# Seven-product feed-forward: two operand sums kept in PSUM, u's sums on GpSimd, token products by halves in one bank

## The chip, the cores and the metric

One Trainium2 chip, one of its cores. The metric is the device time of one launch in microseconds, as the median of the runs shown. A core has TensorE (PE in the profile; its weight loads are a row of their own, PEld), VectorE (DVE), ScalarE (ACT), GpSimd (POOL) and the queues that issue DMAs, SyncE's (SP) and ScalarE's among them. Each engine runs its own instructions in program order and waits on semaphores for the others.

## The reference

`x` is 8 sequences of 3008 tokens with 256 channels. A spectral filter (FFT over the tokens, a complex 256x256 product with bias, a soft threshold, inverse FFT) feeds a mixer:

```python
X = np.fft.rfft(x, axis=1)
Yr = Xr @ w_r - Xi @ w_i + b_r          # Yi likewise, then a soft threshold on both
x = np.fft.irfft(Y, n=x.shape[1], axis=1)
xt = x.transpose(0, 2, 1)
h = np.maximum(xt @ w_tok1, 0.0) @ w_tok2
u = x + h.transpose(0, 2, 1)
h2 = np.maximum(u @ w_ch1, 0.0) @ w_ch2
return (u + h2).astype(np.float32)
```

## The kernel before

Everything is kept transposed, channels on partitions and tokens in the free dimension. An fp32 product is made of three matmuls on halves of the words (`mm3`, lines 196 to 198: high by high, high by low, low by high), so every operand is first split into a high part (a cast, on ACT, line 146 or `high`, line 1112) and a low part (the value less its high part, line 149 or `lower` and `above`).

**Stages.** Until about 1125 us the spectral filter of all five units runs beside the feed-forward of the first two sequences. From then on `channel7` does the remaining six sequences, three units of two, in 18 chunks. A chunk is 1024 tokens wide (896 for the first of a unit) and is worked as two halves of h = 512 (448) columns. `u @ w_ch1` and the product with `w_ch2` are each seen as 2x2 blocks (two halves of the 256 channels by two halves of the tokens, and so on) and made with seven block products instead of eight. The operands of the first are seven sums of quarters of u (`b11`, `t1`, `t2`, `b21`, `b22`, `t3`, `t4`), split into high and low in tiles `ub`; those of the weights are made once, by `weigh` and `weigh2`.

**A step.** Each chunk has six steps, one for each pair of hidden blocks. `one(new, i)` makes first-layer product i, on the PSUM banks x, w and y (tiles `sx`, `sw`, `sy` in the profile); products 6, 7 and 4 add to bank x and product 3 to bank w. From the banks come the four blocks of the hidden layer and, after the ReLU, the seven operands of the second layer: `b11`, `b22`, `b21` and the sums `t1`, `t2`, `t4`, `t3` (tiles `ts`; the split operands are `op`). `two(old, i)` makes the second-layer products of the step before: 1, 5, 6, 7 and 2 gather in banks of their own (`po`), 3 and 4 go to bank y and are added to `uf` at once (`taken`). At a chunk's last step (`ends`) the gathered sums are added to `uf` and stored.

**Between the steps.** `make_u` (line 844) makes u for a group of up to 470 tokens: two halves of 128 channels, twelve large matmuls and some small ones, in bank x for the first half and bank y for the second, each copied by ACT to `uf` (line 867). The table `when` sets one group behind each of two or three steps of a chunk. `first_u` and `rest_u` (lines 1027 to 1042) make the operands of the next chunk behind the last two steps: four sums on DVE, and seven splits by `divide`, high on ACT and low on DVE.

**Order.** The program is written engine by engine in this order, and a scheduler then sets the order of the instructions on each engine, so products of the step before slip in between those of the new one. At run time each engine takes its list as it stands.

Two things in the code matter below. A PSUM bank is used by one engine at a time: the next writer or reader of bank x on another engine waits for the last. And `sn`, `ts`, `op`, `ub` are rings of 4, 4, 9 and 8 buffers.

Of the kernel before, what the change touches and what calls it, by code (L numbers as in the profile page):

```python
# [11 lines left out]
F32 = mybir.dt.float32  # L12
# [3 lines left out]
ALU = mybir.AluOpType  # L16
# [110 lines left out]
def tile_kernel(ctx: ExitStack, tc: tile.TileContext, io):  # L127
# [716 lines left out]
    def make_u(g):  # L844
        u, b, s0, k = groups[g]
        gh, gl = gts[u]
        w, b2 = wts.pop(g), b2s.pop(g)
        _, c0, c1 = span(g)
        n = c1 - c0
        homes = [m for m, (cu, at, cw) in enumerate(chunks) if cu == u and at < c1 and c0 < at + cw]  # L850
        for m in homes:
            if m not in ufs:
                ufs[m] = wc["uf"].tile([128, 2, CW7 if chunks[m][2] > CW else CW], F32, name="uf", bufs=3)
        for ct in range(2):
            cs = slice(ct * 128, (ct + 1) * 128)
            pt = wc["banks"]["xy"[ct]] if "banks" in wc else bank("pu")
            for jt in range(2):
                mm3(pt[:, :n], gh[:, jt, b, cs], gl[:, jt, b, cs], w[:, jt, :n], w[:, 2 + jt, :n], jt == 0, False)
            for s in range(k):
                PE.matmul(pt[:, s * TOKS:(s + 1) * TOKS], lhsT=b2[:, s, cs], rhs=g2[:, 0 if s0 + s == 0 else 1], start=False, stop=s == k - 1)  # L860
            if g == 0:
                us[0] = [wc["wk2"].tile([128, 2, CW], F32R, name=k) for k in ("uh", "ul")] if ct == 0 else us[0]
                S.copy(out=us[0][0][:, ct, :n], in_=pt[:, :n])
            for m in homes:
                _, at, cw = chunks[m]
                lo, hi = max(at, c0), min(at + cw, c1)
                S.copy(out=ufs[m][:, ct, lo - at:hi - at], in_=pt[:, lo - c0:hi - c0])
            if g == 0:
                V.tensor_tensor(out=us[0][1][:, ct, :n], in0=ufs[0][:, ct, :n], in1=us[0][0][:, ct, :n].bitcast(F32), op=ALU.subtract)
        return n  # L870
# [156 lines left out]
    def first_u(n):  # L1027
# [36 lines left out]
    def channel7(ns):  # L1064
# [46 lines left out]
        def high(new, k, src=None):  # L1111
            S.activation(out=new[3][k][:, 0], in_=new[4][k] if src is None else src, func=AF.Relu if k in ("b11", "b21") else AF.Copy)  # L1112
# [206 lines left out]
```

## Time and profile before

| | |
|---|---|
| median of 3 runs | 2544.31 us (2542.53 to 2550.55) |
| the profiled execution's own time | 2546.06 us |
| its span, first to last instruction | 2544.3 us |
| TensorE clock granted, mean | 0.989 |
| busy: PE, PEld | 2374.4 us (93%), 1988.2 us (78%) |
| busy: DVE, ACT, POOL | 1831.6 us (72%), 1398.1 us (55%), 1216.3 us (48%) |
| first product of `channel7` starts | 1125.4 us |
| DMA: HBM read, written | 177.57 MB, 97.39 MB |

A row of the groups of instructions gives the line, the engine, out<-in by the program's names, the shape, how often, busy time and mean duration in ns, and the idle time before with what ended it. A row of the timeline gives start and duration in us, and in brackets the idle time before and what ended it. Durations of matmuls overlap, so a matmul's price is read from start to start. A row of the waits gives who waited for whom, the total in us, how often, and the longest.

### The profile page before, as it was taken

What the parts mean: (1) busy time and instruction counts of PE and PEld (TensorE: products, weight loads), DVE (VectorE), ACT (ScalarE), POOL (GpSimd) and SP (SyncE); (2) the same over time, 40 slices, a digit from 0 to 9 for tenths busy, and PEclk for the clock granted to TensorE, in tenths of its full rate; (3) what the DMA queues carried; (4) which work ended last, traced back from release to release, by engine and by line L of the source; (5) the groups of instructions that cost most, each with busy time, mean ns of one, the idle gap of its engine ahead of it and who ended that gap; (6) DMA issues with size and microseconds to landing.
All of it is one profiled execution on the core that took longest, in us unless ns stands there. A gap on an engine that the chain in (4) does not pass through costs nothing.

```text
span 2544.3 us, 33504 instructions
## 1 busy us (share of the span) xinstructions
PE 2374.4 (93%) x12200; PEld 1988.2 (78%) x12200; DVE 1831.6 (72%) x2551; ACT 1398.1 (55%) x2492; POOL 1216.3 (48%) x905
## 2 busy tenths in 40 slices
PE   8999999999999999998998989989989899998887
PEld 7778989999888889887776767777767677776665
DVE  7876667655466645566788887788787878777886
ACT  6754445445344434345665665665665666665564
POOL 0001332323133323315767676676677766776766
PEclk9999999999999999998999999999999999999999
DMA  8864577656555554341121112212112121221100
GB/s 210 255 217 131 178 232 225 176 171 199 176 172 170 162 166 141 116 134 37 56 63 59 37 56 63 63 47 86 42 36 71 44 82 37 61 63 35 54 1 33
DMA packets 149762, 277.13 MB, mean 109 GB/s; under 512 B 10917, under 2 KB 94461, under 8 KB 149597
## 3 DMA queue, kind: packets, MB, share of 16 engines
q1 hardware_dynamic: 115209, 208.40, 27.8%
q10 hardware_dynamic: 34388, 66.60, 7.7%
q8 instruction: 96, 1.57, 0.3%
q14 instruction: 69, 0.57, 0.1%
HBM read 177.57 MB, written 97.39 MB: 108 GB/s over the span
## 4 chain that ended last, share of the span: by engine, by line
PE 44%; DVE 17%; POOL 15%; issue 14%; ACT 4%; DMA 3%; SPq 1%; DVEq 0%; ACTq 0%; POOLq 0%
POOL op L1101 11%; DVE sn L1101 3%; PE po L197 3%; PE po L196 3%; PE po L198 3%; POOL ts L1101 3%; PE px L482 2%; DVE ts L1101 2%; PE ph L196 2%; PE pm L198 2%; PE pm L196 2%; PE ph L198 2%; PE ph L197 2%; PE pm L197 2%; DVE ts L1104 2%
## 5 line engine op out<-in xcount | busy, mean ns | idle before, releaser
L1101 POOL TENSOR_TENSOR op<-ts,op 128x512 fp32r<-128x512 f32 (+1 forms) x432 | 618.1, 1451 | 0.0
L1112 ACT ACTIVATE op<-ts 128x512 fp32r<-128x512 f32 (+1 forms) x432 | 264.9, 619 | 257.8 <-DVE ts L1104 107.2
L1101 POOL TENSOR_TENSOR op<-sn,op 128x512 fp32r<-128x512 f32 (+1 forms) x108 | 166.4, 1541 | 493.7 <-ACT op L1112 439.2
L149 POOL TENSOR_TENSOR yl<-z,yh 128x512 fp32r<-128x512 f32 x72 | 95.9, 1332 | 272.6 <-ACT yh L146 266.5
L485 POOL TENSOR_TENSOR xf<-xf 128x256 f32<-128x256 f32 x84 | 68.6, 816 | 242.0 <-ACT xf L484 216.1
L1112 ACT ACTIVATE op<-sn 128x512 fp32r<-128x512 f32 (+1 forms) x216 | 134.6, 623 | 80.2 <-DVE sn L1101 77.2
L1101 DVE TENSOR_TENSOR sn<-sy,sn 128x512 f32<-128x512 f32 (+1 forms) x108 | 73.1, 676 | 139.0 <-ACT sn L1108 84.6
L149 DVE TENSOR_TENSOR xtl<-xf,xth 128x768 fp32r<-128x768 f32 x84 | 85.1, 1013 | 118.4 <-ACT xth L146 118.3
L1108 ACT COPY sn<-sx 128x512 f32<-128x512 f32 (+1 forms) x216 | 123.6, 572 | 60.2 <-PE sx L198 58.2
L899 DVE SCALAR_TENSOR_TENSOR hlo<-ph,hh 128x512 fp32r<-128x512 f32 (+3 forms) x156 | 98.6, 636 | 77.5 <-ACT hh L898 77.1
L196 PE MATMUL pm<-wmh,xth 128*128 128x256 f32 x504 | 146.1, 290 | 4.9 <-ACT xth L146 3.0
L1101 DVE TENSOR_TENSOR uf<-sy,uf 128x512 f32<-128x512 f32 (+1 forms) x216 | 144.8, 671 | 6.5 <-PE sy L198 6.4
L1101 POOL TENSOR_TENSOR ts<-sn 128x512 f32<-128x512 f32 (+1 forms) x108 | 148.9, 1379 | 0.0
L198 PE MATMUL pm<-wmh,xtl 128*128 128x256 f32 x504 | 142.4, 284 | 0.8 <-DVE xtl L149 0.8
L197 PE MATMUL pm<-wml,xth 128*128 128x256 f32 x504 | 142.3, 283 | 0.0
L898 ACT ACTIVATE hh<-ph 128x512 fp32r<-128x512 f32 (+3 forms) x156 | 86.3, 556 | 99.6 <-PE ph L198 91.5
L1101 DVE TENSOR_TENSOR ts<-sn,ts 128x512 f32<-128x512 f32 (+1 forms) x108 | 126.5, 1172 | 8.4 <-ACT op L1112 0.5
L196 PE MATMUL po<-op,ws 128*128 128x512 f32 (+1 forms) x324 | 128.9, 398 | 3.4 <-ACT op L1112 1.5
L197 PE MATMUL po<-op,ws 128*128 128x512 f32 (+1 forms) x324 | 128.3, 396 | 3.9 <-POOL op L1101 3.9
L1104 DVE SCALAR_TENSOR_TENSOR op<-sn,op 128x512 fp32r<-128x512 f32 (+1 forms) x108 | 107.5, 995 | 31.1 <-ACT op L1112 31.1
L198 PE MATMUL po<-op,ws 128*128 128x512 f32 (+1 forms) x324 | 127.4, 393 | 0.0
L196 PE MATMUL ph<-uh,w 128*128 128x512 f32 (+3 forms) x312 | 117.8, 379 | 3.8 <-DVE hlo L899 2.9
(243 smaller groups left out, 7592.4 us busy)
## 6 DMA issues: line engine op xcount, KB each, us to landing
wt<-wt_d SPq DMA_DIRECT2D x28, 940.0 KB, 5.7
x<-in_x SPq DMA_DIRECT2D x39, 480.0 KB, 4.6
wt<-ws_d SPq DMA_DIRECT2D x36, 512.0 KB, 4.4
a<-a_d SPq DMA_DIRECT2D x36, 512.0 KB, 5.6
b_d<-bt ACTq DMA_DIRECT2D x36, 512.0 KB, 5.7
a_d<-a ACTq DMA_DIRECT2D x36, 480.0 KB, 4.0
wt<-wt_d SPq DMA_DIRECT2D x21, 752.0 KB, 5.0
b<-b_d SPq DMA_DIRECT2D x32, 480.0 KB, 6.3
```

Source lines behind the costliest of these rows:

```text
L149: lo_eng.tensor_tensor(out=lo, in0=src, in1=hi.bitcast(F32), op=ALU.subtract)
L196: PE.matmul(out, lhsT=wh, rhs=xh, start=start, stop=False, skip_group_check=more)
L197: PE.matmul(out, lhsT=wh, rhs=xl, start=False, stop=False, skip_group_check=more)
L198: PE.matmul(out, lhsT=wl, rhs=xh, start=False, stop=stop, skip_group_check=more)
L482: PE.matmul(pt[:, o:o + 128], lhsT=x, rhs=f2cols(2 * kp + ab), start=True, stop=True)
L485: (V if plain else G).tensor_tensor(out=xf[:, 0], in0=xf[:, 1], in1=xf[:, 2], op=ALU.add)
L898: S.activation(out=hh, in_=pt, func=AF.Relu)
L899: V.scalar_tensor_tensor(out=hlo, in0=pt, scalar=0.0, in1=hh.bitcast(F32), op0=ALU.max, op1=ALU.subtract)
L1101: eng.tensor_tensor(out=out, in0=in0, in1=in1, op=op)
L1104: V.scalar_tensor_tensor(out=out, in0=in0, scalar=0.0, in1=in1, op0=MAX, op1=op)
L1108: S.copy(out=t, in_=banks[k][:, :new[2]])
L1112: S.activation(out=new[3][k][:, 0], in_=new[4][k] if src is None else src, func=AF.Relu if k in ("b11", "b21") else AF.Copy)
```

## The change

- **The sums in PSUM.** The first products' copies (`snap`) stay, but the sums for b11 and b22 are written back to banks y and w instead of to SBUF, and their ReLU copies on ACT go. `t1`, `t2` and the new `t3` are made by one DVE instruction each that takes the ReLU while it reads the bank; the low parts of b11 and b22 likewise. `t3` and b22's low part move from POOL to DVE. b21 is copied to SBUF by ACT with the ReLU, and its low part moves from DVE to POOL.
- **The order of products.** `two(old, 3)` comes ahead of `one(new, 6)`; 3 goes ahead of 2; `one(new, 4)` and what hangs on it come behind `two(old, 2)`.
- **Token products by halves.** `half_u` makes one half of a group, always in bank x, and the table sets one half (in a unit's first chunk two) behind a step; groups are fetched behind their second half.
- **u's sums on GpSimd.** Within `channel7` the low parts of `ub` and the sums `t1` to `t4` of u go to POOL. `weigh` and `weigh2` take their scratch from a pool of their own instead of from the `ub` ring.

```diff
-            pt = wc["banks"]["xy"[ct]] if "banks" in wc else bank("pu")
+        pt = wc["banks"]["x"] if "banks" in wc else bank("pu")
...
-        pool, w1 = wc["seven"], wc["w1"]
-        a = pool.tile([128, 2, 2, 2, 128], F32, tag="ub", name="a", bufs=8)
+        pool, w1 = wc["sums"], wc["w1"]
+        a = pool.tile([128, 2, 2, 2, 128], F32, tag="a", name="a")
...
-        split(ub[:, 0], ub[:, 1], src, S, V)
+        split(ub[:, 0], ub[:, 1], src, S, G if "tail" in wc else V)
...
-        V.tensor_tensor(out=t1, in0=b12, in1=b11, op=ALU.subtract)
+        (G if "tail" in wc else V).tensor_tensor(out=t1, in0=b12, in1=b11, op=ALU.subtract)
...
             if new:
+                sums(new, "t1", "t2", "t4", "t3")
+                X, W, Y = (b[k][:, :h] for k in "xwy")
                 one(new, 1)
-                v["b11"] = snap(new, "x")
-                one(new, 5)
-                v["b22"] = snap(new, "w")
+                x1 = snap(new, "x")
             if old:
                 two(old, 1)
...
             if new:
-                one(new, 6)
-                v["x2"] = snap(new, "x")
-                one(new, 2)
-                add(v["b11"], b["y"][:, :h], v["b11"])
-                high(new, "b11")
-                one(new, 3)
-                add(v["x2"], b["w"][:, :h], v["x2"])
-                S.activation(out=v["x2"], in_=v["x2"], func=AF.Relu)
-                one(new, 7)
-                add(v["b22"], b["x"][:, :h], v["b22"])
-                S.activation(out=v["b22"], in_=v["b22"], func=AF.Relu)
-                high(new, "b22")
+                one(new, 5)
+                w1 = snap(new, "w")
             if old:
                 two(old, 3)
                 taken(old, 3, 1)
             if new:
-                sums(new, "t1", "t2", "t4", "t3")
-                above(v["t1"], v["b11"], v["x2"], SUB)
-                add(v["t2"], v["b22"], v["t1"])
+                one(new, 6)
+                x2 = snap(new, "x")
+                one(new, 3)
+                add(x2, W, x2)
+                S.activation(out=x2, in_=x2, func=AF.Relu)
+                one(new, 2)
+                add(Y, Y, x1)
+                high(new, "b11", Y)
+                one(new, 7)
+                add(W, X, w1)
+                above(v["t1"], Y, x2, SUB)
+                high(new, "b22", W)
+                lower(new, "b11", Y)
+                above(v["t2"], W, v["t1"], ADD)
                 high(new, "t1")
             if old:
                 two(old, 5)
-            if new:
-                one(new, 4)
-                high(new, "b21", b["x"][:, :h])
-                above(v["t4"], b["x"][:, :h], v["t2"], SUB)
-                above(new[3]["b21"][:, 1], b["x"][:, :h], new[3]["b21"][:, 0].bitcast(F32), SUB)
-                high(new, "t2")
-                high(new, "t4")
-                lower(new, "t1")
-                add(v["t3"], v["b22"], v["x2"], G, SUB)
-                above(new[3]["b11"][:, 1], v["b11"], new[3]["b11"][:, 0].bitcast(F32), SUB)
-                high(new, "t3")
-                for k in ("b22", "t2", "t4", "t3"):
-                    lower(new, k)
...
+            if new:
+                one(new, 4)
+                v["b21"] = single()[:, :h]
+                S.activation(out=v["b21"], in_=X, func=AF.Relu)
+                above(v["t4"], X, v["t2"], SUB)
+                high(new, "b21")
+                lower(new, "b22", W)
+                above(v["t3"], W, x2, SUB)
+                high(new, "t2")
+                high(new, "t4")
+                high(new, "t3")
+                for k in ("t1", "b21", "t2", "t4", "t3"):
+                    lower(new, k)
...
-                spots = [(m - 2, half - len(mine) + 1 + i) for i in range(len(mine) - 1)] + [(m - 1, 3)]
+                spots = [(m - 2, half - 2), (m - 2, half - 1), (m - 1, 0), (m - 1, 1)][4 - 2 * len(mine[1:]):] + [(m - 1, 2), (m - 1, 3)]
```

What the scheduler makes of it, at three places. First DVE in one step without token products, from the addition that takes bank w's sum to the two `taken` (in the names, `sn<-sw,sn` is that addition, `op` a low part, `ts` a sum). Before:

```order
L1101 TENSOR_TENSOR sn<-sy,sn 128x512
L1104 SCALAR_TENSOR_TENSOR op<-sn,op 128x512
L1101 TENSOR_TENSOR sn<-sw,sn 128x512
L1101 TENSOR_TENSOR sn<-sx,sn 128x512
L1101 TENSOR_TENSOR uf<-sy,uf 128x512
L1104 SCALAR_TENSOR_TENSOR ts<-sn 128x512
L1101 TENSOR_TENSOR ts<-sn,ts 128x512
L1101 TENSOR_TENSOR uf<-sy,uf 128x512
L1104 SCALAR_TENSOR_TENSOR ts<-sx,ts 128x512
L1104 SCALAR_TENSOR_TENSOR op<-sx,op 128x512
```

And after:

```order
L1111 TENSOR_TENSOR sn<-sw,sn 128x512
L1111 TENSOR_TENSOR sy<-sy,sn 128x512
L1111 TENSOR_TENSOR sw<-sx,sn 128x512
L1114 SCALAR_TENSOR_TENSOR ts<-sy,sn 128x512
L1114 SCALAR_TENSOR_TENSOR op<-sy,op 128x512
L1114 SCALAR_TENSOR_TENSOR ts<-sw,ts 128x512
L1114 SCALAR_TENSOR_TENSOR op<-sw,op 128x512
L1114 SCALAR_TENSOR_TENSOR ts<-sx,ts 128x512
L1114 SCALAR_TENSOR_TENSOR ts<-sw,sn 128x512
L1111 TENSOR_TENSOR uf<-sy,uf 128x512 x2
```

Ten instructions become eleven, and the three that read SBUF alone (`op<-sn,op`, `ts<-sn`, `ts<-sn,ts`) are gone: each of the eleven reads a bank. The second place is PE around the token products of a chunk's later step (`sx<-wt`, `sy<-wt` and the small `g`, `b` products are a group's two halves). Before:

```order
L196 MATMUL po<-op,w2h 128x512
L197 MATMUL po<-op,w2h 128x512
L196 MATMUL sx<-wt_14397,gh 128x470
...
L860 MATMUL sx<-g_79,b_14399 128x94 x5
L196 MATMUL sy<-wt_14397,gh 128x470
...
L860 MATMUL sy<-g_79,b_14399 128x94 x5
L196 MATMUL sx<-ub,w_963 128x448
```

And after:

```order
L198 MATMUL po<-op,ws_10466 128x512
L196 MATMUL sx<-wt_12485,gh 128x470
...
L864 MATMUL sx<-g_79,b_12487 128x94 x5
L196 MATMUL sw<-ub,ws 128x512
L197 MATMUL sw<-ub,ws 128x512
L196 MATMUL po<-op,ws_10466 128x512
L197 MATMUL po<-op,ws_10466 128x512
L198 MATMUL po<-op,ws_10466 128x512
L196 MATMUL sx<-ub,w_963 128x512
```

One half stands there now, and between it and the next step's first product in bank x stand five matmuls on other banks. The third place is POOL from one chunk's `uf<-t` to the next's. Before, each step has six instructions and nothing lies between the steps; after it reads:

```order
L1042 TENSOR_TENSOR t<-uf 128x512
L1111 TENSOR_TENSOR op<-ts,op 128x512
...
L1048 TENSOR_TENSOR t<-uf 128x512
L1049 TENSOR_TENSOR t<-t,uf 128x512
L1050 TENSOR_TENSOR t<-uf,t 128x512
...
L149 TENSOR_TENSOR ub<-t,ub 128x512 x2
L149 TENSOR_TENSOR ub<-uf,ub 128x512 x2
L149 TENSOR_TENSOR ub<-t,ub 128x512 x2
L1111 TENSOR_TENSOR op<-ts,op 128x512
L1111 TENSOR_TENSOR op<-sn,op 128x512
```

A step has five instructions there now (`op<-ts,op`, `op<-sn,op` and three more `op<-ts,op`), and ten of u's low parts and sums stand between the steps, six of them in a row ahead of the low parts of the chunk's last step.

More of the change, by code (lines that the diff above doesn't have):

```diff
@@ L842, in load_b2, with home, half_u @@
         b2s[g] = b2
-    def make_u(g):
+    def home(g):
+        u = groups[g][0]
+        _, c0, c1 = span(g)
+        found = [(m, at, cw) for m, (cu, at, cw) in enumerate(chunks) if cu == u and at < c1 and c0 < at + cw]
+        for m, _, cw in found:
+            if m not in ufs:
+                ufs[m] = wc["uf"].tile([128, 2, CW7 if cw > CW else CW], F32, name="uf", bufs=3)
+        return c0, c1, found
+    def half_u(g, ct):
         u, b, s0, k = groups[g]
         gh, gl = gts[u]
-        w, b2 = wts.pop(g), b2s.pop(g)
-        _, c0, c1 = span(g)
+        w, b2 = wts[g], b2s[g]
+        c0, c1, found = home(g)
@@ L870, in make_u @@
-        return n
+        cs = slice(ct * 128, (ct + 1) * 128)
+        pt = wc["banks"]["x"] if "banks" in wc else bank("pu")
+        for jt in range(2):
+            mm3(pt[:, :n], gh[:, jt, b, cs], gl[:, jt, b, cs], w[:, jt, :n], w[:, 2 + jt, :n], jt == 0, False)
+        for s in range(k):
+            PE.matmul(pt[:, s * TOKS:(s + 1) * TOKS], lhsT=b2[:, s, cs], rhs=g2[:, 0 if s0 + s == 0 else 1], start=False, stop=s == k - 1)
+        if g == 0:
+            us[0] = [wc["wk2"].tile([128, 2, CW], F32R, name=k) for k in ("uh", "ul")] if ct == 0 else us[0]
+            S.copy(out=us[0][0][:, ct, :n], in_=pt[:, :n])
@@ L872, in split_u, with make_u @@
+        for m, at, cw in found:
+            lo, hi = max(at, c0), min(at + cw, c1)
+            S.copy(out=ufs[m][:, ct, lo - at:hi - at], in_=pt[:, lo - c0:hi - c0])
+        if g == 0:
+            V.tensor_tensor(out=us[0][1][:, ct, :n], in0=ufs[0][:, ct, :n], in1=us[0][0][:, ct, :n].bitcast(F32), op=ALU.subtract)
+        if ct:
+            del wts[g], b2s[g]
+    def make_u(g):
+        for ct in range(2):
+            half_u(g, ct)
+        return groups[g][3] * TOKS
     def split_u(n):
@@ L1111, in high, with lower @@
         def high(new, k, src=None):
-            S.activation(out=new[3][k][:, 0], in_=new[4][k] if src is None else src, func=AF.Relu if k in ("b11", "b21") else AF.Copy)
-        def lower(new, k, eng=G):
-            add(new[3][k][:, 1], new[4][k], new[3][k][:, 0].bitcast(F32), eng, SUB)
+            S.activation(out=new[3][k][:, 0], in_=new[4][k] if src is None else src, func=AF.Copy if k[0] == "t" else AF.Relu)
+        def lower(new, k, src=None):
+            lo, hi = new[3][k][:, 1], new[3][k][:, 0].bitcast(F32)
+            if src is None:
+                add(lo, new[4][k], hi, G, SUB)
+            else:
+                above(lo, src, hi, SUB)
         def taken(old, i, q):
```

50 lines of the change are left out of this document (17 added, 33 removed).

## The prediction, on record before the changed kernel ran

> **What bounds the kernel now.** I read the page's head, then the stages, the waits of the later stage, and one step's timeline. The stages first (us, busy time of PE, PEld, DVE, ACT and POOL, granted clock, DMA):
>
> ```profile
> 150.00:1125.00 975.00, 960.34 (x5704) 867.75 (x5703) 596.13 (x889) 450.07 (x770) 252.33 (x218) 1.00 0.56 172
> 1125.00:2544.30 1419.30, 1278.84 (x5747) 1007.87 (x5745) 1114.20 (x1409) 848.97 (x1545) 962.48 (x682) 0.98 0.17 52
> 1175.00:1200.00 25.00, 16.94 (x50) 11.64 (x49) 17.29 (x27) 10.34 (x21) 8.64 (x7) 0.71 0.00 0
> ```
>
> Until 1125 us PE is full, and the change touches nothing there but `weigh`'s scratch. In the 1419 us of `channel7` every engine has idle time: PE 140 us by busy time, and more in truth, since a matmul's shown end overlaps the next. So I count PE by starts. A 512-wide matmul starts every 0.23 us, a 448-wide one every 0.205, and one half of a 470-token group takes 2.42 us (1602.95 to 1605.37):
>
> ```profile
> 1611.89 0.40 PE L196 MATMUL po<-op,ws 128*128 128x512 f32 x1
> 1612.12 0.39 PE L197 MATMUL po<-op,ws 128*128 128x512 f32 x1
> 1612.35 0.39 PE L198 MATMUL po<-op,ws 128*128 128x512 f32 x1
> ...
> 1612.90 0.36 PE L197 MATMUL sx<-ub,w 128*128 128x448 f32 x1
> 1613.11 0.36 PE L198 MATMUL sx<-ub,w 128*128 128x448 f32 x1
> ```
>
> ```profile
> 1602.95 0.48 PE L196 MATMUL sx<-wt,gh 128*128 128x470 f32 x1 [0.69 <-DVE op L1104]
> ...
> 1605.37 0.46 PE L196 MATMUL sy<-wt,gh 128*128 128x470 f32 x1
> ...
> 1605.62 0.55 ACT L867 COPY uf<-sx 128x470 f32<-128x470 f32 x1 [0.87 <-PE sx L860]
> ```
>
> A step has 14 products of three matmuls: 42 x 0.23 = 9.66 us, or 8.61 at 448. There are 90 and 18 steps, and by these rows (each half has two such matmuls, and bank y as many as x) 44 halves of 470 tokens and 36 of 376:
>
> ```profile
> L1101 DVE TENSOR_TENSOR sn<-sy,sn 128x512 f32<-128x512 f32 x90 | 61.9, 687 | 106.4 <-ACT sn L1108 61.8 <-PE sy L198 44.5
> L196 PE MATMUL sx<-wt,gh 128*128 128x470 f32 x44 | 18.5, 420 | 17.0 <-DVE op L1104 17.0
> L196 PE MATMUL sx<-wt,gh 128*128 128x376 f32 x36 | 13.6, 379 | 6.9 <-DVE op L1104 6.9
> ```
>
> PE's floor: 90 x 9.66 + 18 x 8.61 + 44 x 2.42 + 36 x 1.95 (scaled by width) = 869 + 155 + 106 + 70 = **1200 us** of 1419. The other 219 us are what the change can win. Who keeps PE waiting, from 1300 to 2480 us (total, times, longest):
>
> ```profile
> PEld sx L196 <- DVE op L1104: 54.9, 48, 2.7
> PEld sx L196 <- ACT sn L1108: 47.4, 108, 1.3
> PEld sy L196 <- DVE uf L1101: 30.7, 27, 2.0
> PEld sy L196 <- DVE sn L1101: 24.6, 20, 1.9
> ```
>
> Nearly all waits are for a bank (x, y) that DVE or ACT still reads. Why DVE is late shows in one step:
>
> ```profile
> 1684.75 1.79 DVE L1101 TENSOR_TENSOR ts<-sn,ts 128x512 f32<-128x512 f32 x1
> ...
> 1685.96 1.72 POOL L1101 TENSOR_TENSOR op<-ts,op 128x512 fp32r<-128x512 f32 x1
> ...
> 1687.00 0.68 DVE L1104 SCALAR_TENSOR_TENSOR ts<-sx,ts 128x512 f32<-128x512 f32 x1
> 1687.60 0.68 DVE L1104 SCALAR_TENSOR_TENSOR op<-sx,op 128x512 fp32r<-128x512 f32 x1
> 1687.64 1.28 POOL L1101 TENSOR_TENSOR ts<-sn 128x512 f32<-128x512 f32 x1
> ...
> 1688.33 0.50 PE L196 MATMUL sx<-ub,w 128*128 128x512 f32 x1 [1.53 <-DVE op L1104]
> ...
> 1689.48 0.57 ACT L1108 COPY sn<-sx 128x512 f32<-128x512 f32 x1
> ```
>
> `ts<-sn,ts` reads only SBUF and takes 1.79 us beside POOL, whose instruction takes 1.72; with a bank as DVE's input they take 0.68 and 1.28. DVE's next comes 0.60 after such a start. PE waits 1.53 us at the end of that chain, for bank x. By groups:
>
> ```profile
> L1101 DVE TENSOR_TENSOR ts<-sn,ts 128x512 f32<-128x512 f32 x90 | 108.9, 1211 | 6.6 <-ACT op L1112 0.5
> L149 DVE TENSOR_TENSOR ub<-t,ub 128x512 fp32r<-128x512 f32 x60 | 81.2, 1374 | 27.4 <-ACT ub L146 22.1 <-PE sx L198 5.3
> L149 DVE TENSOR_TENSOR ub<-uf,ub 128x512 fp32r<-128x512 f32 x45 | 71.7, 1615 | 3.5 <-ACT ub L146 3.5
> L1104 DVE SCALAR_TENSOR_TENSOR ts<-sx,ts 128x512 f32<-128x512 f32 x90 | 61.4, 682 | 3.8 <-ACT op L1112 0.8
> ```
>
> ```profile
> L1101 POOL TENSOR_TENSOR op<-ts,op 128x512 fp32r<-128x512 f32 x360 | 524.4, 1477 | 0.0
> L1101 POOL TENSOR_TENSOR op<-sn,op 128x512 fp32r<-128x512 f32 x90 | 141.4, 1571 | 358.7 <-ACT op L1112 358.7
> ```
>
> **The sums in PSUM.** All eleven of DVE's instructions in a step now read a bank: 11 x 0.60 = 6.6 us of 9.66, where the list before has ten with three that swell. The rule against this stands in the Trainium skill, "VectorE: DVE Perf Modes", Rules for kernel authors: copy a matmul's output to SBUF first if many operations follow. It does not hold in the trace, where SBUF inputs cost 1.21 to 1.62 and a bank 0.68; by it, the sum would go towards the first rival below. ACT loses the two ReLU copies and gains b21's: twelve instructions a step as before. What the trace lacks is DVE writing to a bank. I bound one by a bank read, 0.60, and by the 1.21 of `ts<-sn,ts`, and take 0.60, the row with a bank in it.
>
> Does a step then hold 9.66 us? In the new order, with `one(1)` starting at 0 and 0.69 a product, `one(7)` ends at 4.8. ACT's copies of x (0.57 each) fall between `one(1)`, `one(6)` and `one(7)`, where other banks' products stand. A bank's readers come one after the other, which this place shows (DVE waits for ACT's read of x):
>
> ```profile
> 1132.31 0.52 ACT L1112 ACTIVATE op<-sx 128x448 fp32r<-128x448 f32 x1
> ...
> 1132.87 0.62 DVE L1104 SCALAR_TENSOR_TENSOR ts<-sx,ts 128x448 f32<-128x448 f32 x1 [0.88 <-ACT op L1112]
> ```
>
> So: w's sum from 5.0, ACT's high parts of b11 until 5.65 and of b22 until 6.3, `t1` 5.7, b11 low 6.3, `t2` 6.9, b22 low 7.5, `t4` from 8.1 to 8.8, `t3` to 9.4, `taken` to 10.0. Banks x, w, y are free at 8.8, 9.4, 10.0; the next step wants them at 9.66, 10.35, 11.0. Each has about 0.8 us to spare, so a plain step runs at PE's rate. POOL: the last low part, `t3`, is done near 13.5, and its product comes at 9.66 + 8.2 = 17.9.
>
> **Token products by halves.** The same matmuls. In bank x a half is wanted 8.5 us after `one(1)`, and x is free at 8.4: no room. The copy to `uf` (0.55 us, two of them where a group straddles chunks) is covered by the five matmuls on other banks that stand behind it in the list. I take 0.3 us for each of 74 halves (0 to 1), **22 us**. A group's loads go to SP's queue behind its second half:
>
> ```profile
> wt<-wt_d SPq DMA_DIRECT2D x28, 940.0 KB, 5.7
> ...
> b<-b_d SPq DMA_DIRECT2D x32, 480.0 KB, 6.3
> ```
>
> They land in 5.7 and 6.3 us, and the next half comes a step later, 9.66 us or more; the store ahead of them on the queue waits for POOL's `uf<-t` of a step before. That step covers them, so I cost them at nothing; without the cover each group would add up to 6.
>
> **u's sums on POOL.** DVE loses eleven instructions a chunk at 1.37 to 1.62. POOL gets 760 instructions where the stage has 682, at 1.28 because hardly a DVE instruction without a bank is left (two `uf<-t` a chunk): 973 us, under PE's 1200. What counts is its queue: three sums stand ahead of step 4's low parts, six of u's low parts ahead of step 5's. Step 4's are done 3.9 us into step 5, the six at 11.7, then step 5's at 13.0 (`t1`) to 19.5 (`t3`, with one more of u's between), against PE's wants at 14.4 to 17.9: 1.5 us late. DVE's seven extra instructions at a chunk's end and ACT's six casts in step 5 push x by another 0.5 to 1. I take 2.5 us for each of 17 chunk changes (0 to 5), **43 us**.
>
> The Trainium skill, "GPSIMD Engine Reference", Engine selection, speaks against the move: elementwise work belongs on VectorE, GpSimd being about twice as slow. The rows give that ratio (1.28 to 0.68). By the rule, with this time exposed, 11 x 0.6 x 17 = 112 us would be lost and the sum 2527; its mechanism here is the second rival.
>
> `weigh` keeps off the `ub` ring, whose delay shows at 1175 to 1200 (PE busy 16.94 of 25, clock 0.71); that stall is no part of the floor and goes. For the stage's first and last step, where nothing fills the waits, I add **25 us** (10 to 40).
>
> **Sum.** 1200 + 22 + 43 + 25 = 1290 us for the stage instead of 1419: 2544.3 - 129 = 2415. The profiled execution took 2546.06 with a span of 2544.3, the median of the runs is 2544.31; the 1.8 us between are within the runs' scatter. So **2415 us**; its own range, from the bounds (stage 1225 to 1350), is 2350 to 2475.
>
> **Rivals.** *DVE pays more for banks*: two writes a step at 1.21 put `t4` 1.2 us later. Plain steps lose 0.4, and the 74 with a half 1.1: 34 x 0.4 + 74 x 1.1 = 95 us, 2510 at most, 2490 in the middle. For it: no row has such a write. Against: PSUM reads cost what SBUF reads cost uncontended.
>
> *Slower, by POOL's queue at the chunk change.* If POOL's instructions stay at 1.72 there, step 4's five, the nine and step 5's five are 19 x 0.44 = 8.4 us later, so PE waits about 10 instead of 1.5: 17 x 8.4 = 143 more, 2558. It decides from 7.6 us more a change, or 1.68 an instruction. For it: the mean of `op<-ts` is 1477 ns already. Against: 1.28 beside a bank-reading DVE, and POOL idles 358.7 us for ACT.
>
> *No change*: the list, made for other durations than the chip's, puts each saved wait in front of another bank, as the table of waits has four kinds of them: 2544.
>
> **Chances.** Forecast 0.66; banks dearer 0.18 (2475 to 2510); no change 0.05; slower 0.08; better than 2350, 0.03. The range 2350 to 2500 leaves out the last three and part of the second. Faster 0.87, within 0.3% (about what a measurement of this kernel can tell from no change) 0.05, slower 0.08.
>
> **What would show it.** Right: DVE's `ts` and `op` groups all near 680 ns and POOL's `op<-ts` near 1290; PE's starts 9.7 us a plain step; the waits for bank x in tenths of a microsecond; stalls left at the chunk changes, PE waiting for POOL's `op`; the clock at 1.00 from 1175 on. Wrong: `sy<-sy,sn` or `sw<-sx,sn` well over 700 ns; PE waiting for `ub` or `op` of POOL for several microseconds a chunk; or half products waiting on bank x for more than 1 us.

## The result, and the profile after

| | before | after |
|---|---|---|
| median of 4 runs | 2545.06 us | **2400.65 us** (2399.15 to 2403.79) |
| ratio, 95% interval | | 0.9431 [0.9412, 0.9451] |
| the profiled span | 2544.3 us | 2400.3 us |

144 us less; 2415 (2350 to 2500) was predicted. The stages of the changed kernel, in the columns of the prediction's first fence:

```profile
150.00:1125.00 975.00, 957.34 (x5679) 864.04 (x5678) 595.42 (x887) 449.36 (x769) 251.88 (x218) 1.00 0.56 172
1125.00:2400.30 1275.30, 1242.53 (x5770) 1000.22 (x5768) 844.44 (x1333) 848.19 (x1546) 955.96 (x761) 1.00 0.19 58
1175.00:1200.00 25.00, 24.82 (x116) 20.78 (x114) 17.74 (x32) 20.13 (x41) 19.67 (x17) 1.00 0.17 48
```

All of it is in `channel7`: PE idles 33 us there by busy time instead of 140, DVE is busy 844 us instead of 1114, POOL and ACT as long as before. The stall at 1175 and the low clock are gone. The mean of 0.98 over 1419 us is some 28 us of clock, but much of that passed while PE waited anyway. By the timeline of the kernel before, 79 matmuls of the stage run late for the clock alone, without a wait (those of 512 columns start 0.43 us apart instead of 0.23, those of 448 start 0.375 instead of 0.204, as at 1197.62 and 1197.99): some 14 us of the 144. In the changed kernel no matmul does. So the clock alone is not the gain; whether PE's waits brought it down was not tried. The groups of instructions on the two engines that the change is about:

```profile
L1111 DVE TENSOR_TENSOR sy<-sy,sn 128x512 f32<-128x512 f32 x90 | 62.8, 698 | 0.0
L1111 DVE TENSOR_TENSOR sw<-sx,sn 128x512 f32<-128x512 f32 x90 | 62.9, 699 | 0.1
L1114 DVE SCALAR_TENSOR_TENSOR ts<-sw,sn 128x512 f32<-128x512 f32 x90 | 61.2, 680 | 0.0
L1111 POOL TENSOR_TENSOR op<-ts,op 128x512 fp32r<-128x512 f32 x360 | 467.8, 1321 | 231.3 <-ACT op L1122 202.4 <-PE po L198 18.2 <-PE sx L198 10.7
```

A DVE instruction that writes a bank takes 698 ns, one that only reads one 680; POOL's low part takes 1321 instead of 1477. Who keeps PE waiting (1300 to 2340 us; like the prediction's window, it ends some 60 us ahead of the span's end):

```profile
PEld sx L196 <- ACT sn L1118: 27.0, 82, 1.6
PEld sx L196 <- DVE sw L1111: 18.0, 59, 0.6
...
PE po L196 <- DVE uf L1111: 9.2, 15, 0.9
...
PEld sy L196 <- DVE op L1114: 6.1, 17, 0.6
```

Before, the first rows were 54.9 and 47.4. To see which steps still lose, I take the start of DVE's addition in bank y as the mark of a step; the timeline's first and last such rows, and two of plain steps (with DVE's next instruction behind one of them, of which more below):

```profile
1134.10 0.62 DVE L1111 TENSOR_TENSOR sy<-sy,sn 128x448 f32<-128x448 f32 x1
...
2353.78 0.70 DVE L1111 TENSOR_TENSOR sy<-sy,sn 128x512 f32<-128x512 f32 x1
2354.47 0.70 DVE L1111 TENSOR_TENSOR sw<-sx,sn 128x512 f32<-128x512 f32 x1
...
2363.08 0.70 DVE L1111 TENSOR_TENSOR sy<-sy,sn 128x512 f32<-128x512 f32 x1
2381.84 0.70 DVE L1111 TENSOR_TENSOR sy<-sy,sn 128x512 f32<-128x512 f32 x1
```

The 107 steps between take 1247.7 us. PE's work in them, at the start-to-start times that most matmuls of this trace have (0.2275 and 0.204 us), is 89 x 42 x 0.2275 + 18 x 42 x 0.204 + 44 x 2.42 + 36 x 1.95 = 1181.3. So 66.4 us are lost; by the same marks the kernel before loses 214.6 in the same steps. Of the 66.4, 13.8 stand in a chunk's steps 1 to 4, and 52.7 in the two steps around the 17 chunk changes, 3.1 a change. One such change, ACT, POOL, PE, DVE and PE again:

```profile
1836.66 1.29 POOL L1111 TENSOR_TENSOR op<-ts,op 128x512 fp32r<-128x512 f32 x1
1837.91 1.29 POOL L1111 TENSOR_TENSOR op<-sn,op 128x512 fp32r<-128x512 f32 x1
...
1839.23 0.59 ACT L1118 COPY sn<-sx 128x512 f32<-128x512 f32 x1 [1.91 <-POOL op L1111]
...
1839.87 0.50 PE L196 MATMUL sx<-ub,ws 128*128 128x512 f32 x1 [0.63 <-ACT sn L1118]
1840.21 0.39 PE L197 MATMUL sx<-ub,ws 128*128 128x512 f32 x1
...
1843.62 1.88 DVE L1111 TENSOR_TENSOR uf<-po,uf 128x512 f32<-128x512 f32 x3
...
1845.05 0.47 PE L196 MATMUL po<-op,w2h 128*128 128x512 f32 x1 [0.79 <-DVE uf L1111]
```

ACT's copy of bank x wants an `sn` buffer that POOL's low part of b21 (`op<-sn,op`) still reads, and that instruction stood behind six low parts of u. PE stands for bank x meanwhile. Five microseconds later it stands again, for the chunk-end additions (`uf<-po,uf`) that read the banks of the sums.

### The profile page after: what moved, and what is told of

The parts are those of the page before. It is cut to its first block, busy times and chain, and to the rows that moved or that the text cites. A ratio compares the mean times of both kernels' runs of the same rounds, so it can differ in the third digit from the quotient of the medians.

```text
span 2400.3 us, 33632 instructions
## 1 busy us (share of the span) xinstructions
PE 2335.2 (97%) x12200; PEld 1976.1 (82%) x12200; DVE 1561.3 (65%) x2472; ACT 1395.7 (58%) x2492; POOL 1209.3 (50%) x984
## 4 chain that ended last, share of the span: by engine, by line
PE 74%; DVE 8%; POOL 5%; ACT 4%; issue 4%; DMA 4%; SPq 1%; ACTq 0%; DVEq 0%; POOLq 0%
PE po L196 6%; PE po L197 6%; PE po L198 6%; PE sx L196 5%; PE sx L197 4%; PE sx L198 4%; PE sx L864 3%; POOL op L1111 3%; PE px L482 2%; PE sy L196 2%; PE sy L197 2%; PE sy L198 2%; PE ph L196 2%; PE pm L198 2%; PE pm L196 2%
## 5 line engine op out<-in xcount | busy, mean ns | idle before, releaser
L1111 POOL TENSOR_TENSOR op<-ts,op 128x512 fp32r<-128x512 f32 (+1 forms) x432 | 550.2, 1296 | 343.5 <-ACT op L1122 310.5
L196 PE MATMUL pm<-wmh,xth 128*128 128x256 f32 x504 | 146.1, 290 | 5.1 <-ACT xth L146 3.0
L1111 DVE TENSOR_TENSOR sn<-sw,sn 128x512 f32<-128x512 f32 (+1 forms) x108 | 73.5, 680 | 118.1 <-PE sw L198 75.6
L197 PE MATMUL pm<-wml,xth 128*128 128x256 f32 x504 | 142.3, 283 | 0.0
L1111 POOL TENSOR_TENSOR op<-sn,op 128x512 fp32r<-128x512 f32 (+1 forms) x108 | 137.8, 1276 | 0.0
L196 PE MATMUL po<-op,ws 128*128 128x512 f32 (+1 forms) x324 | 126.2, 389 | 0.0
L197 PE MATMUL po<-op,ws 128*128 128x512 f32 (+1 forms) x324 | 125.9, 388 | 0.2 <-POOL op L1111 0.2
L198 PE MATMUL po<-op,ws 128*128 128x512 f32 (+1 forms) x324 | 125.4, 387 | 0.0
L146 ACT CAST xth<-xf 128x768 fp32r<-128x768 f32 x84 | 70.2, 835 | 89.2 <-POOL xf L485 89.2
L196 PE MATMUL ph<-uh,w 128*128 128x512 f32 (+3 forms) x312 | 118.4, 380 | 2.9 <-DVE hlo L908 2.0
L197 PE MATMUL po<-hlo,w2h 128*128 128x512 f32 (+3 forms) x312 | 116.3, 373 | 3.2 <-DVE hlo L908 3.2
L196 PE MATMUL po<-hh,w2h 128*128 128x512 f32 (+3 forms) x312 | 116.5, 373 | 2.2 <-ACT hh L907 1.2
L197 PE MATMUL ph<-ul,w 128*128 128x512 f32 (+3 forms) x312 | 116.1, 373 | 0.0
```

Of the source, the lines that this page charges most:

```text
L146: S.copy(out=hi, in_=src)
L196: PE.matmul(out, lhsT=wh, rhs=xh, start=start, stop=False, skip_group_check=more)
L197: PE.matmul(out, lhsT=wh, rhs=xl, start=False, stop=False, skip_group_check=more)
L198: PE.matmul(out, lhsT=wl, rhs=xh, start=False, stop=stop, skip_group_check=more)
L1111: eng.tensor_tensor(out=out, in0=in0, in1=in1, op=op)
```

## The experiments

My theory: the gain comes from DVE's instructions with two SBUF inputs leaving the chain that frees the banks; they and POOL's instructions swell each other. Rivals: the move of u's sums brings it, or the order of products does. Four parts of the change (place of the sums, order of products, token products whole or by halves, u's sums on DVE or POOL) were set one against another. Two smaller edits go along: `weigh`'s own scratch (in every kernel of the table but before and e1) and a fourth buffer in the ring of `t`, which had three (in every one but before). The table orders the runs by that, not by time of running:

| kernel | sums | order | token products | u's sums | median us | ratio to before, 95% interval |
|---|---|---|---|---|---|---|
| before | SBUF | old | whole | DVE | 2545 to 2548 | |
| e1_u_pool | SBUF | old | whole | POOL | 2547.76 | 1.0001 [0.9987, 1.0015] |
| e3_sbuf_sums | SBUF | new | halves | POOL | 2571.56 | 1.0100 [1.0069, 1.0131] |
| e12_psum_only | PSUM | old | whole | DVE | 2405.28 | 0.9442 [0.9423, 0.9461] |
| e14_whole_dve | PSUM | new | whole | DVE | 2407.44 | 0.9458 [0.9437, 0.9478] |
| e2_u_dve | PSUM | new | halves | DVE | 2476.82 | 0.9722 [0.9695, 0.9748] |
| e11_old_order | PSUM | old | halves | POOL | 2421.29 | 0.9502 [0.9472, 0.9532] |
| after | PSUM | new | halves | POOL | 2400.65 | 0.9431 [0.9412, 0.9451] |
| **e5_whole** | PSUM | new | whole | POOL | **2390.89** | 0.9387 [0.9370, 0.9403] |

**The sums back in SBUF** (e3). DVE keeps its order of instructions in the step, seven of its eleven with other operands:

```diff
-                add(Y, Y, x1)
-                high(new, "b11", Y)
+                add(x1, Y, x1)
+                high(new, "b11", x1)
...
-                add(W, X, w1)
-                above(v["t1"], Y, x2, SUB)
+                add(w1, X, w1)
+                above(v["t1"], x1, x2, SUB)
...
-                above(v["t3"], W, x2, SUB)
+                above(v["t3"], w1, x2, SUB)
```

> The changed kernel with its order of DVE's instructions, but b11's and b22's sums written to SBUF and read there by t1, t2, t3 and the two low parts. My theory (a bank as input spares DVE and POOL the mutual slowdown): five of DVE's eleven instructions a step swell from 0.6 to 1.2 or 1.7 us, the list takes 10 to 11 us where a step has 9.6, POOL's low parts go to 1.5 us, and the run ends at 2540 us (2470 to 2640). Rival D (the order of the products brings the gain, not where the sums are kept): 2395 to 2430, with DVE's list hidden.

2571.56 us: 171 more, and slower than before. Groups and a row of the waits:

```profile
L1111 POOL TENSOR_TENSOR op<-ts,op 128x512 fp32r<-128x512 f32 x360 | 528.8, 1487 | 259.1 <-ACT op L1122 239.1 <-PE sx L198 20.1
L1114 DVE SCALAR_TENSOR_TENSOR op<-sn,op 128x512 fp32r<-128x512 f32 x180 | 230.8, 1282 | 0.0
L1114 DVE SCALAR_TENSOR_TENSOR ts<-sn 128x512 f32<-128x512 f32 x180 | 184.2, 1023 | 0.1
...
PEld sx L196 <- DVE ts L1114: 107.0, 63, 4.4
```

The same instructions that take 680 ns with a bank as input take 1282 and 1023 with two SBUF inputs, POOL's low part goes back to 1487, and PE waits for bank x, whose last reader (`t4`) stands behind them on DVE. The list of PE moved too, since the scheduler answers to the other operands; that DVE's list alone costs the 171 us is not shown, that its swollen instructions stand ahead of the bank PE waits for is. The low clock is back as well (0.98): counted as above, some 27 of the 171 us are matmuls that run late without a wait.

**The sums in PSUM alone** (e12). The kernel before with the new operands of the sums (and with them `t3` and b22's low part on DVE, b21's on POOL, `weigh`'s scratch in its own pool; the second layer's product 1 stands one product earlier); the rest as before:

```diff
                 one(new, 2)
-                add(v["b11"], b["y"][:, :h], v["b11"])
-                high(new, "b11")
+                add(Y, Y, x1)
+                high(new, "b11", Y)
...
-                add(v["b22"], b["x"][:, :h], v["b22"])
-                S.activation(out=v["b22"], in_=v["b22"], func=AF.Relu)
-                high(new, "b22")
+                add(W, X, w1)
+                above(v["t1"], Y, x2, SUB)
+                high(new, "b22", W)
```

> The kernel before, with the sums in PSUM (and what goes with them: t3 and b22's low part on DVE, b21's on GpSimd, weigh's scratch in its own pool), the order of products as before, token products whole, u's sums on DVE. If the parts add: 2477 (without u's move) + 21 (old order) - 10 (token products whole) = 2488 us (2475 to 2500), so that the sums in PSUM alone bring 57 of the 144 us. Rival (they don't add: u's low parts on DVE, swollen beside POOL, hold the banks in the old order): 2510 to 2545. Rival (the sums in PSUM bring nearly all by themselves): 2400 to 2440.

2405.28 us, so the second rival: this kernel has 142 of the 144 us, and my sum of parts was off by 83. Some 9 of the 142 belong to `weigh`'s scratch (e6, below), so the sums themselves bring about 133 if the two add up. The fourth `t` buffer was not tried by itself with the sums in PSUM; e1 has it with the sums in SBUF and gains nothing. In the kernels with whole token products the lines are nine lower (1102 for 1111, 1105 for 1114, 1113 for 1122):

```profile
L1102 DVE TENSOR_TENSOR sw<-sx,sn 128x512 f32<-128x512 f32 x90 | 62.7, 697 | 7.2
L1102 POOL TENSOR_TENSOR op<-ts,op 128x512 fp32r<-128x512 f32 x360 | 472.6, 1337 | 406.4 <-ACT op L1113 227.9 <-PE po L198 170.2 <-PE sx L198 8.3
...
PEld po L197 <- POOL op L1102: 24.4, 21, 1.4
```

DVE's and POOL's instructions have the changed kernel's durations in the old order too; of PE's waits, POOL's low parts lead.

**u's sums on GpSimd alone** (e1). The kernel before with

```diff
-        split(ub[:, 0], ub[:, 1], src, S, V)
+        split(ub[:, 0], ub[:, 1], src, S, G if "tail" in wc else V)
```

and the four sums likewise.

> The kernel before, with only u's sums and the low parts of ub moved to GpSimd. My theory (the gain of 144 us comes from DVE's chain that frees banks x, w and y, inside every step): 2500 us (2470 to 2530), since the step keeps its SBUF-only instructions on DVE and POOL's longer list stays swollen beside them. Rival A (u's sums on DVE were the load, and moving them brings most of the gain): 2400 to 2450. Rival B (POOL's queue makes the chunk change later while POOL's instructions are at 1.5 us and more): 2544 to 2600.

2547.76 us: no change, where I expected 44 less. The instructions inside the step are as long as they were or longer, and PE waits for them:

```profile
L1104 DVE SCALAR_TENSOR_TENSOR op<-sn,op 128x512 fp32r<-128x512 f32 x90 | 111.9, 1244 | 19.7 <-ACT op L1112 19.7
L149 POOL TENSOR_TENSOR ub<-uf,ub 128x512 fp32r<-128x512 f32 x45 | 68.7, 1539 | 14.1 <-DVE w2l L149 11.9 <-ACT ub L146 2.2
...
PEld sx L196 <- DVE op L1104: 55.8, 37, 2.7
```

In the kernel before that row is 48.7, 43, 2.7 over the same 1300 to 2340 us. The move was not without effect: PE's wait for DVE's addition in bank y went (`PEld sy <- DVE sn`, 19.1 us before), while this one grew and one for ACT's copy of the token products came up (`PEld sx <- ACT uf`, 12.0 us). So the move took one wait away and others took its place.

**u's sums back on DVE in the changed kernel** (e2, the same lines the other way).

> The changed kernel, with u's sums and low parts back on DVE. My theory: in the chunk changes DVE has eleven SBUF-only instructions of 1.3 to 1.6 us more in two steps, 15 us where its slack is 2 x 3 us, so 5 to 9 us may be lost at 17 changes at most and 2 to 4 are likely: 2450 us (2420 to 2520). Rival A (u's sums brought most of the gain): 2500 and more. Rival C (DVE's slack takes them in, the move was not needed): 2395 to 2410.

2476.82 us, 76 more, within my range. 59 of them stand in the steps around the chunk changes (112.1 us lost there by the marks, against 52.7). One change, DVE, POOL and PE:

```profile
1801.92 1.72 DVE L149 TENSOR_TENSOR ub<-uf,ub 128x512 fp32r<-128x512 f32 x1
1803.56 3.48 DVE L149 TENSOR_TENSOR ub<-t,ub 128x512 fp32r<-128x512 f32 x2
...
1801.80 4.69 POOL L1111 TENSOR_TENSOR op<-ts,op 128x512 fp32r<-128x512 f32 x3
...
1807.69 0.50 PE L196 MATMUL sy<-ub,w 128*128 128x512 f32 x1 [1.41 <-DVE uf L1111]
...
1815.43 0.50 PE L197 MATMUL po<-op,w2h 128*128 128x512 f32 x1 [2.01 <-POOL op L1111]
```

Three low parts of u take 5.2 us on DVE beside three of POOL's at 1.56, and DVE's next reader of bank y comes after them. By e12, though, DVE bears the same low parts at 2405. The difference had to be the order or the halves.

**The new order without halves, u's sums on DVE** (e14: e2 with the token products of e5, below).

> The changed kernel with token products whole at the old places and u's sums and low parts on DVE: the new order of products and the sums in PSUM are all that stays of its step. With halves, u's sums on DVE cost 76 us; with whole groups in the old order the same list of DVE's ends at 2405. My theory (a whole group behind a chunk's last step gives PE 4.84 us of work that needs no ub just while DVE makes the next chunk's low parts, and the halves took that cover away): 2405 us (2391 to 2425). Rival (the new order of products is what can't bear u's sums on DVE): 2455 to 2480.

2407.44 us, as my theory had it. The chunk change here, PE and DVE:

```profile
1835.07 0.50 PE L197 MATMUL po<-op,w2h 128*128 128x512 f32 x1 [1.06 <-POOL op L1102]
1835.64 0.33 PE L196 MATMUL sx<-wt,gh 128*128 128x376 f32 x1
...
1837.48 0.42 PE L196 MATMUL sy<-wt,gh 128*128 128x376 f32 x1
...
1834.93 2.38 DVE L149 TENSOR_TENSOR ub<-t,ub 128x512 fp32r<-128x512 f32 x2
```

A whole token group stands behind the chunk's last step and keeps PE busy from 1835.64 to 1839.4 with work that needs neither `ub` nor DVE, just while DVE makes the low parts. With halves instead, the same list costs 69 us more (e2 less e14), and u's sums on GpSimd bring that back (e2 less after: 76). That the halves cost it by taking this cover away is read from the timeline; the runs rule out the rival, the order, which by itself is worth nothing here (e14 against e12: 2.2 us, the intervals overlap).

**Token products whole** (e5). `make_u` and its table as before:

```diff
-                spots = [(m - 2, half - 2), (m - 2, half - 1), (m - 1, 0), (m - 1, 1)][4 - 2 * len(mine[1:]):] + [(m - 1, 2), (m - 1, 3)]
+                spots = [(m - 2, half - len(mine) + 1 + i) for i in range(len(mine) - 1)] + [(m - 1, 3)]
...
-        pt = wc["banks"]["x"] if "banks" in wc else bank("pu")
+            pt = wc["banks"]["xy"[ct]] if "banks" in wc else bank("pu")
```

> The changed kernel with token products whole again (banks x and y, one group behind a step, at the old places). My theory (a half in bank x hides behind five matmuls on other banks, a whole group needs x and y at once, and y is free last): 1 us lost for each of 40 groups, 2440 us (2415 to 2480). Rival (once the banks are free on time the halves bring nothing): 2395 to 2410.

2390.89 us: 10 less, the intervals of the two ratios apart. I expected 40 more. With the sums in PSUM bank y is nearly free in time: of the waits that I thought of the largest is

```profile
PEld sy L196 <- DVE op L1105: 18.8, 28, 1.1
```

and a chunk's steps 1 and 2, which carry no token product now, lose nothing by the marks. This is the fastest kernel of the study.

**The old order in the changed kernel** (e11).

```diff
                 one(new, 5)
                 w1 = snap(new, "w")
-            if old:
-                two(old, 3)
-                taken(old, 3, 1)
             if new:
                 one(new, 6)
...
+                two(old, 3)
+                taken(old, 3, 1)
                 two(old, 5)
```

and likewise 2 ahead of 3, and `one(new, 4)` with what hangs on it ahead of `two(old, 2)`.

> The changed kernel with the sums in PSUM, but the step's products in the order of the kernel before: product 3 of the second layer behind the first layer's product 7, product 2 ahead of 3, product 4 ahead of the second layer's 2. My theory: bank y holds b11's sum until its low part is read, so the second layer's product 3 waits 1 to 2 us a step in bank y: 2500 us (2450 to 2620). Rival (the sums in PSUM suffice in any order): 2395 to 2430.

2421.29 us: 21 more, not 100, and within the rival's range. The wait that I expected each step, for b11's low part in bank y, is not there (`PEld sy <- DVE op` is 2.6 us in 8 waits, against 6.1 in the changed kernel). Two others are, each about once a chunk or less. At a chunk's end product 4 follows product 3 in bank y and waits until `taken` has added 3 to `uf`. And PE waits for a sum's bank behind a DVE instruction that was held. The rows of the waits, then DVE, POOL and PE at one such place:

```profile
PEld sy L196 <- DVE uf L1111: 16.4, 14, 1.3
PEld po L196 <- DVE t L1111: 14.2, 7, 2.4
...
1792.36 3.61 DVE L1111 TENSOR_TENSOR uf<-t,uf 128x512 f32<-128x512 f32 x1
...
1790.35 3.82 POOL L1111 TENSOR_TENSOR op<-ts,op 128x512 fp32r<-128x512 f32 x3
1794.09 1.33 POOL L149 TENSOR_TENSOR ub<-uf,ub 128x512 fp32r<-128x512 f32 x1
...
1796.75 0.50 PE L196 MATMUL po<-op,ws 128*128 128x512 f32 x1 [1.49 <-DVE t L1111]
```

`uf<-t,uf`, with two SBUF inputs, lasts until POOL stops (1795.42; DVE is through at 1795.97), and `t<-po,t`, which frees the bank, stands behind it. This happens nine times in the run (2.52 to 3.83 us) and costs PE 14.4 us. So some two thirds of the 21 us are the delay between DVE and POOL, which this order runs into, and not a bank that it holds longer.

**What is left at the chunk change: one more `sn` buffer** (e7).

```diff
-            return tail.tile([128, CW], F32, tag="sn", name="sn", bufs=4)
+            return tail.tile([128, CW], F32, tag="sn", name="sn", bufs=5)
...
-            return wc["tail"].tile([128, CW], F32, tag="t", name="t", bufs=4)[:, :chunks[n][2] // 2]
+            return wc["tail"].tile([128, CW], F32, tag="t", name="t", bufs=3)[:, :chunks[n][2] // 2]
```

> The changed kernel with five sn buffers instead of four, paid for by three t buffers instead of four. In the trace of the changed kernel ACT's copy of bank x waits at each chunk change for POOL's low part of b21, which stands behind six low parts of u and holds an sn buffer (21.5 us in 11 waits between 1300 and 2340), and PE loses about 1.0 us there. My theory (this wait is what is left of POOL's queue at the chunk change): 17 x 0.9 less, 2385 us (2378 to 2394). Rival (bank x or the short t ring takes the wait over): 2397 to 2405.

2422.65 us (2412.17 to 2435.35), ratio 0.9515 [0.9488, 0.9541]: slower by 22 at the median, by 11 in the profiled span. PE's wait for ACT's copy of x fell from 27.0 to 14.6 us, as meant. In its place came `PEld po L197 <- POOL op`, 14.6, and four stalls of 2.3 to 2.6 us of which this is one, from the timelines of DVE, POOL and PE:

```profile
1849.65 4.95 DVE L1111 TENSOR_TENSOR uf<-t,uf 128x512 f32<-128x512 f32 x1
...
1847.79 2.57 POOL L1111 TENSOR_TENSOR op<-ts,op 128x512 fp32r<-128x512 f32 x2
1850.29 1.31 POOL L1111 TENSOR_TENSOR op<-sn,op 128x512 fp32r<-128x512 f32 x1
1851.53 2.52 POOL L1111 TENSOR_TENSOR op<-ts,op 128x512 fp32r<-128x512 f32 x2
...
1855.86 0.50 PE L196 MATMUL sw<-ub,ws 128*128 128x512 f32 x1 [2.54 <-DVE ts L1114]
```

POOL ran without a gap here, and DVE's one instruction with two SBUF inputs was held until POOL stopped (at 1854.05; DVE was through at 1854.60). Behind it stood `t3`, the last reader of bank w. The run changes two rings at once, so that the freed wait and not the shorter `t` ring brought this about is likely and not shown.

**Another pairing of the banks of the sums** (e8).

```diff
-        total = {1: pair[0][:, 0], 5: pair[0][:, 1], 6: pair[1][:, 0], 7: pair[1][:, 1], 2: bank("po")}
+        total = {2: pair[0][:, 0], 5: pair[0][:, 1], 6: pair[1][:, 0], 7: pair[1][:, 1], 1: bank("po")}
```

> The changed kernel with the banks of the second layer's sums paired anew: product 1 has a tile of its own and 2 shares one with 5, instead of 1 with 5. In the trace of the changed kernel PE waits at the start of a chunk's second step for DVE's additions of bank 5's sum before it writes bank 1 (14.2 us at 17 chunk changes). My theory (the tile of two banks is freed as one, and bank 1 is wanted first): 17 x 0.8 less, 2387 us (2380 to 2395). Rival (DVE's additions are late for the next product in any pairing): 2397 to 2405.

2406.52 us, 0.9446 [0.9430, 0.9462]: nothing gained. PE's wait for DVE's additions is smaller (`PE po L196 <- DVE uf` is 2.8 us in 8 waits, against 9.2 in 15), and another stands beside it (`PE po L197 <- POOL op`, 3.5 us in 2). By the marks 56.4 us are lost around the changes, against 52.7.

**Two of u's low parts back on DVE** (e9, on e5: b21's and b22's).

```diff
-        split(ub[:, 0], ub[:, 1], src, S, G if "tail" in wc else V)
+        split(ub[:, 0], ub[:, 1], src, S, G if "tail" in wc and k not in ("b21", "b22") else V)
```

> The changed kernel with whole token products (2391 us) and the low parts of u's b21 and b22 on DVE instead of GpSimd. My theory (what is left at a chunk change is POOL's queue, for which the waits removed by the fifth sn buffer and by the other pairing of banks only made room): two of its six low parts in a row less is 2.6 us earlier, PE gains 0.5 to 1.5 us at 17 changes: 2376 us (2365 to 2386). Rival (DVE's low parts read SBUF alone, take 1.3 to 1.6 us beside POOL and hold banks x, w and y): 2392 to 2420.

2431.68 us, 0.9549 [0.9530, 0.9568]: 41 more than e5, against my theory. PE waits for POOL's operands more than before, not less (5.5 us in e5's row of this wait):

```profile
1845.80 1.82 DVE L149 TENSOR_TENSOR ub<-uf,ub 128x512 fp32r<-128x512 f32 x1
...
1842.83 5.93 POOL L149 TENSOR_TENSOR ub<-t,ub 128x512 fp32r<-128x512 f32 x4
...
PEld po L197 <- POOL op L1102: 42.9, 29, 2.3
```

Four of POOL's low parts take 1.48 each beside DVE's two, which stand ahead of DVE's readers of the banks, and those make what ACT and POOL work on next. That the last link makes POOL late is read from the order, not tried.

**b21's low part on DVE** (e4: from bank x, as before the change, without ACT's copy).

```diff
-                v["b21"] = single()[:, :h]
-                S.activation(out=v["b21"], in_=X, func=AF.Relu)
-                above(v["t4"], X, v["t2"], SUB)
-                high(new, "b21")
+                high(new, "b21", X)
+                above(v["t4"], X, v["t2"], SUB)
+                lower(new, "b21", X)
```

> The changed kernel with b21's low part back on DVE from bank x, without ACT's copy: DVE has twelve instructions of 0.6 us a step, POOL four. My theory: the sn wait at the chunk change goes (about 15 us less), bank x is free 0.6 us later, which the plain steps hide and the 74 steps with a half don't quite (0.2 to 0.5 us each, 15 to 37 us more): 2410 us (2390 to 2430). Rival (bank x has no spare time, as the step's schedule with 0.8 us to spare was too good): 2440 and more. Rival (bank x has more than 0.6 us to spare everywhere): 2380 to 2390.

2483.85 us, 0.9751 [0.9734, 0.9768]: 83 more; by its size the first rival. The added instruction reads a bank and costs 0.68 like the others, but every step is late, plain ones at 10.6 us. The largest wait is another than the rival names:

```profile
1927.68 0.68 DVE L1114 SCALAR_TENSOR_TENSOR op<-sy,op 128x512 fp32r<-128x512 f32 x1
...
1928.41 0.50 PE L196 MATMUL sy<-op,w2h 128*128 128x512 f32 x1 [0.20 <-DVE op L1114]
```

A product in bank y, for which b11's low part is still read (47.3 us in 84 waits, against 6.1 in 17), then POOL's and ACT's operands. The scheduler had moved products, so this run does not tell bank x's spare time from the other order; that stays open.

**`weigh`'s scratch alone** (e6: the kernel before with its own pool for it).

> The kernel before, with weigh's and weigh2's scratch in a pool of their own. My theory: the stall at 1175 to 1200 (PE busy 16.94 of 25 us at a clock of 0.71) goes, 8 to 12 us less, of which the work ahead of 1125 takes back up to 5: 2537 us (2530 to 2543). Rival (a wait for bank x or y follows at once): 2541 to 2548.

2538.35 us, 0.9966 [0.9955, 0.9977]: about 9 us, as expected. The row of the stall, PE 16.94 and clock 0.71 before:

```profile
1175.00:1200.00 25.00, 21.84 (x108) 18.59 (x107) 20.42 (x28) 16.48 (x32) 17.95 (x16) 1.00 0.00 1
```

## Why the prediction was right, and where its steps were not

- **PE's floor**, 1200: 1191 by the starts of most matmuls (0.2275, not 0.23). A plain step does run at PE's rate: 9.25 to 9.5 us from mark to mark, between which 41 or 42 matmuls start.
- **A DVE write to a bank**, taken at 0.60 of 0.60 to 1.21, from start to start: the next instruction starts some 0.68 later (2353.78 to 2354.47), so two writes cost 0.16 us a step more than the sum has. The first rival's condition, 1.21, fell with that.
- **All of DVE's step on banks**: the step that carries the result. e12 and e3 show it from both sides, some 133 us for it by itself and 171 against it with all else in place. The rows by which SBUF inputs cost 1.21 to 1.62 were among the dearest: `op<-sn,op` and `ts<-sn` of the same list have 1021 and 801 ns, so three instructions swell by 0.1 to 0.5 us. ACT loses one ReLU copy, b22's (b11's ReLU was in its cast), and not two; its twelve instructions a step are right. The rule to copy matmul output to SBUF first if many operations follow (the Trainium skill, "VectorE: DVE Perf Modes", Rules for kernel authors) has its nearest trial in e3, which keeps the sums in SBUF, and loses here; the same row leaves it open to take PSUM as the source. The Trainium skill, "SBUF — State Buffer", Who interferes with whom, gives a reason beside GpSimd: a DVE instruction with two SBUF inputs contends with a GpSimd instruction that reads SBUF, one with at most one such input (outside the modes that use two ports) does not. The traces agree (1282 and 1023 ns against 680; POOL 1487 against 1321). What the prediction's rows show as reading only SBUF is this rule's two SBUF inputs.
- **The new order**, on whose schedule the prediction built 0.8 us of spare time a bank: worth nothing with whole groups (e12, e14), 21 us with halves, of which 14.4 are the held `uf<-t,uf` of e11. It was not needed for the gain.
- **Halves**, 22 us: 13.8 are lost in steps 1 to 4, where 57 of the 80 halves stand, so the size was right. So was the place: the next product waits for the half's copy out of bank x (`PEld sx <- ACT uf`, 14.5 us in 53 waits). The mistake was not to price the whole group in the new step, which costs 10 less (e5).
- **u's sums on GpSimd**, 43 us at 17 changes: 52.7 are lost there, but PE does not wait for POOL's `op` as the step said. It waits for ACT's copy, held by POOL through an `sn` buffer, and for DVE's additions; that the size came near is luck. In e7 a wait for POOL's `op` took the place of the first of these; e8 lessened the second, and no time was won. What the move itself is worth depends on the neighbours: 0 us with the sums in SBUF (e1), 16.5 with whole groups (e5 against e14), 76 with halves. The Trainium skill's rule for elementwise work ("GPSIMD Engine Reference", Engine selection) by which the sum came to 2527 did not decide. The ratio of two that the prediction took is to a DVE instruction with a bank; u's own sums and low parts have means of 0.69 to 1.08 us on DVE (e14) and 1.29 to 1.30 on POOL (e5), and with the sums in PSUM the kernel is 16.5 to 76 us faster with them there.
- **The ends**, 25 us: 1274.9 of the stage, from 1125.4 on, less 1191, 13.8 and 52.7, leave 17.4, of which 5.1 pass before the first product (1130.5).
- **Slower by POOL's queue**: its condition, 1.68 us an instruction, was not met (1.32). The low clock and the stall at 1175 went; the stall was worth about 9 us (e6).

So the total came out right, 1275 instead of 1290 for the stage, with one part of four behind it. The mechanism of that part was the prediction's. The other three together change nothing clear of the scatter (2405.28 for e12, 2400.65 after, the intervals overlap): the halves cost what the move of u's sums gives back. The prediction priced the change as a whole, so its number could not show that one part is enough.

## What to carry to other kernels

Ask of each DVE instruction beside a busy GpSimd how many of its inputs lie in SBUF: keeping one input in PSUM, even by writing a sum back to its bank, took some 133 us off 2545 here. Price a group of edits part by part, since two of them can cancel, and before spreading large products over many steps see what they cover where they stand. A wait that is taken away at a crowded place shows only the next one (e7, e8), so count the queue behind it first.

## What was not expected of the hardware

- The mutual delay has no bound of one instruction: `uf<-t,uf` took 4.95 us while POOL ran four instructions without a gap, and the like happened four times in e7 (4.74 to 4.96) and nine times in e11 (2.52 to 3.83), where the longest in the changed kernel is 1.63. In both places shown DVE was through 0.55 us after POOL stopped. The Trainium skill ("SBUF — State Buffer", Summary: rules for kernel authors) has the second one to issue blocked until the first finishes. The 1.72 and 1.79 of the kernel before look like a wait for one instruction, these thirteen do not. Why DVE got in after one instruction elsewhere and not here, no run tells.
- A wait of PE costs more than itself: the matmul after a late one starts 0.31 to 0.34 us behind it instead of 0.23 (1839.87 to 1840.21 is one).
